# Weight conversion in one VectorE pass, wider loads, a second u buffer and later stores in a fused attention and SoLU kernel

## Chip, cores and metric

The kernel runs on one core of a Trainium2 chip. The metric is the device time of one execution in microseconds (us). All arithmetic is float32; the two weight matrices arrive as 64-bit floats and are converted on the chip.

## The reference

```python
# attention: batch 8, heads 8, seq 576, head_dim 64
scores = scale * q @ k^T                              # 576 x 576 for each head
thresh = max(scores) - tau
scores = where(scores >= thresh, scores, -1e9)
attn   = exp(scores - max) / (sum + 1e-9)
a      = attn @ v
# bridge: (B, H, S, D) -> x of 4608 tokens x 512
h   = x @ w_in                                        # 4608 x 1024
sm  = exp(h - max(h)) / (sum + 1e-9)
u   = h * sm
ln  = (u - mean(u)) / sqrt(var(u) + 1e-6) * g_ln
out = ln @ w_out                                      # 4608 x 512
```

## The kernel before

The five engines are TensorE (PE, matmuls), VectorE (DVE), ScalarE (ACT), GpSimd (POOL) and SyncE (SP, which issues most DMA transfers). Each works through its own queue in the order in which the program emits the instructions. The program is one loop over rounds `rnd`; the order inside a round is written out by hand, and lists (`begin`, `middle`, `late`, `load_at`) hold jobs for later rounds.

The first 144 rounds (`NS`) each take one attention slot: 128 query rows of two heads. PE makes the scores (L401), DVE the row maxima (L417), ACT a threshold ramp (L432) and the exponentials (L442), all on the same two PSUM tiles, so the scores of the next round wait for the ramp of this one. One round later POOL divides by the row sums (`normalise`, L449 to L452) and DVE transposes the result in blocks of 32 into T (`blocks`, L464). After every second slot SP moves T into wT with four SBUF to SBUF transfers (L475), and three or more rounds later PE multiplies with v (`attend`, L500).

When a group of tokens is complete, its feed-forward tiles (36 in all, 128 tokens each) run between the slots: h on PE in two halves (L543, L552); in `late` of that round the max hm (L565, DVE) and the exponential into u (`ff_exp`, L571, ACT); a round later the product h * u (L577, DVE); then statistics (L592, L593, DVE), small scalar work (L596 to L603, POOL), one normalised copy into V (L613, ACT) and one in u itself (L618, DVE). `ff_swap` exchanges 32-row blocks by four transfers from u into V (L629), `ff_turn` transposes V into uT (L640, DVE), and PE multiplies uT by w2 into o (L652) in two rounds. `ff_out` copies o to ob (L670, ACT) and stores it with two transfers (L676). There is one u buffer and one V buffer. After round 144 only feed-forward tiles are left; then uT alternates between two buffers.

The weights are converted in the first 16 rounds, one piece x of 128 x 512 per round: pieces 0 to 7 are w_in, 8 to 15 w_out. Three raw buffers hold pieces as they arrive. `weight_load(x + 3)` is emitted in round x: one transfer for w_in (L203), four of 32 rows for w_out (L208), each `piece(x)[0][r, g]` of the view

```python
w_rows = w_out.rearrange("(g c r x) n -> c r g x n", g=2, r=2, x=32)
```

`weight_a(x + 1)`, in round x, takes the exponent and the mantissa bits apart on DVE (L219, L225) and scales the exponent on ACT (L224). `weight_b(x)` joins low word and mantissa (L239) and sign and exponent (L242) on DVE. `weight_c(x)`, one round later, multiplies by the unit (L251) and by the power of two (L254) on POOL. `weight_d(x)`, two rounds after `weight_b`, copies a w2 piece with its halves exchanged (L261); `w2_done` after the last one allows the first o. In round 2, g_ln is turned into a column by PE (L175, L176).

`load_v` brings v for four heads: each half of the partitions gets all 512 main tokens, in two transfers of 256 tokens (L146), and the last 64 tokens (L150). Both halves hold the same data; `attend` uses the lower half for one pair of heads and the upper half for the other.

Of the kernel before, what the change touches and what calls it, by code (L numbers as in the profile page):

```python
# [8 lines left out]
F32 = mybir.dt.float32  # L9
# [4 lines left out]
ALU = mybir.AluOpType  # L14
AX = mybir.AxisListType
PSUM = bass.MemoryType.PSUM
P = 128
# [3 lines left out]
def kernel(  # L21
# [27 lines left out]
    nc = tc.nc  # L49
    B, H, S, D = q.shape  # L50
    DM, DFF = w_in.shape
    SM = 512
# [6 lines left out]
    ROWS = (slice(0, 64), slice(64, P))  # L59
# [21 lines left out]
    wide = w_in.dtype == I64  # L81
# [12 lines left out]
    ffn = {}  # L94
# [43 lines left out]
    def load_v(b, hf):  # L138
        d = halves.setdefault((b, hf), {})
        hs = slice(4 * hf, 4 * hf + 4)  # L140


        d["v"] = loads.tile([P, 4, NK, D], F32, tag="v", bufs=3, name="v")
        for rows in ROWS:
            for r in range(2):
                nc.sync.dma_start(  # L146
                    out=d["v"][rows, :, 4 * r : 4 * r + 4].rearrange("p h t d -> p h (t d)"),
                    in_=v[b, hs, 256 * r : 256 * r + 256, :].rearrange("h (p t) d -> p h (t d)", t=4),
                )
            nc.sync.dma_start(  # L150
                out=d["v"][rows, :, NK - 1], in_=v[b, hs, SM:S, :].rearrange("h p d -> p h d")
            )
# [33 lines left out]
    def piece(x):  # L186
        if x < 2 * NP:
            c, hf = divmod(x, 2)
            cols = slice(512 * hf, 512 * hf + 512)
            return w_in[P * c : P * c + P, cols], w1[:, c, cols], W_UNIT  # L190
        c = x - 2 * NP
        return w_rows[c], w2[:, 2 * c], gs[:, c : c + 1]
# [4 lines left out]
    def weight_load(x):  # L197
        raw = work.tile(
            [P, 512], I64 if wide else F32, tag=("xh2", "xh3", "uT")[x % 3], bufs=1, name="raw"
        )  # L200
        queue = nc.scalar if x < 3 else nc.sync
        if x < 2 * NP:
            queue.dma_start(out=raw, in_=piece(x)[0])  # L203
        else:
            for r in range(2):
                for g in range(2):
                    o = 64 * r + 32 * g
                    queue.dma_start(out=raw[o : o + 32], in_=piece(x)[0][r, g])  # L208
        raws[x] = dict(raw=raw)

    def weight_a(x):
# [16 lines left out]
        )  # L228

    def weight_b(x):  # L230
        d = raws[x]
        _, dst, unit = piece(x)
        if not wide:
            nc.vector.tensor_scalar(out=dst, in0=d["raw"], scalar1=unit, scalar2=None, op0=ALU.mult)
            return
        words = d["raw"].bitcast(I32).rearrange("p (n two) -> p n two", two=2)
        lo, hi = words[:, :, 0], words[:, :, 1]
        e, m = d["em"]
        nc.vector.scalar_tensor_tensor(  # L239
            out=dst, in0=lo.bitcast(U32), scalar=2.0**-32, in1=m, op0=ALU.mult, op1=ALU.add  # L240
        )
        nc.vector.scalar_tensor_tensor(  # L242
            out=e, in0=hi, scalar=-(2**31), in1=e, op0=ALU.bitwise_and, op1=ALU.bitwise_or
        )

    def weight_c(x):
        d = raws.pop(x)
        _, dst, unit = piece(x)
        if not wide:
            return  # L250
        nc.gpsimd.tensor_scalar(  # L251
            out=dst, in0=dst, scalar1=unit, scalar2=1.0, op0=ALU.mult, op1=ALU.mult
        )
        nc.gpsimd.tensor_tensor(out=dst, in0=dst, in1=d["em"][0].bitcast(F32), op=ALU.mult)  # L254


    def weight_d(x):
        c = x - 2 * NP
        if c >= 0:
            for r in range(2):  # L260
                nc.sync.dma_start(out=w2[ROWS[r], 2 * c + 1], in_=w2[ROWS[1 - r], 2 * c])  # L261
# [217 lines left out]
    def attend(key):  # L479
        b, kind, hp = key  # L480
        unit = units[key]
        wT = unit["wT"]
        unit["y"] = take("pv")
        _, y = unit["y"]
        y = y.rearrange("p (u n) -> p u n", u=2)

        for e in range(2) if kind == 2 else [None]:
            for m in range(NK):
                for u in range(2):
                    d, h0 = source(b * NP + (hp if e is None else e + 2 * u))  # L490
                    for h in range(2):
                        if e is None:
                            to = y[ROWS[h], u, 0:P].rearrange("p (r g x) -> p g r x", r=2, g=2)
                            rhs = wT[ROWS[u], :, m, :, h]
                        else:
                            to = y[ROWS[h], u, 64 * e : 64 * e + 64].rearrange(
                                "p (g x) -> p g x", g=2
                            )
                            rhs = wT[ROWS[u], :, m, e, h]
                        nc.tensor.matmul(  # L500
                            out=to, lhsT=d["v"][ROWS[u], h0 + h, m], rhs=rhs,
                            start=m == 0, stop=m == NK - 1,
                        )

# [61 lines left out]

    def ff_exp(t):
        d = ffn[t]
        d["u"] = work.tile([P, DFF], F32, tag="u", bufs=1, name="u")
        d["se"] = small.tile([P, 1], F32, tag="se", name="se")  # L570
        nc.scalar.activation(  # L571
            out=d["u"], in_=d["h"], func=AF.Exp, bias=d["nm"], scale=1.0, accum_out=d["se"]
        )
# [59 lines left out]

    def ff_turn(t, rnd):
        d = ffn[t]

        turns.append(t)
        tag = "xh0" if rnd > NS and len(turns) % 2 else "uT"
        d["uT"] = uT = work.tile([P, 2 * NC, 2, 32], F32, tag=tag, bufs=1, name="uT")
        nc.vector.transpose(  # L640
            out=uT, in_=d["V"].rearrange("p y (m x) -> p m y x", x=32)
        )
        d["turned"] = rnd + 1
# [13 lines left out]
                    )  # L657

    def ff_out(t):
        d = ffn.pop(t)  # L660
        ob = work.tile([P, DM], F32, tag="ob", name="ob")
        if len(t) == 1:
            rows = out.rearrange("(b s) m -> s b m", s=S)[SM:S, 2 * t[0] : 2 * t[0] + 2]
        else:
            b, kind, m = t
            rows = out[b * S : b * S + SM, :].rearrange("(p t) m -> t p m", t=4)
            rows = rows[2 * kind + m].rearrange("(r k) m -> k r m", r=2)


        nc.scalar.copy(  # L670
            out=ob.rearrange("p (r n) -> p r n", r=2),
            in_=d["o"].rearrange("p (r n) -> p r n", r=2)[:, :, 0:256],
        )
        pairs_free.append(d["otag"])
        for z in range(2):
            nc.sync.dma_start(  # L676
                out=rows[:, :, 256 * z : 256 * z + 256],
                in_=ob[ROWS[z]].rearrange("p (r n) -> p r n", r=2),
            )


# [34 lines left out]
    with tc.manual_schedule():  # L716
# [20 lines left out]
        rnd = 0  # L737
        prev = cur = None

        between, turns = [], []  # L740
        quarter = 0
        w2_done = False

# [1 line left out]
        while True:  # L745
# [45 lines left out]
                whole_pair(whole[rnd])  # L791
            if rnd - 1 in live:
                normalise(rnd - 1)
            if rnd - 1 in pieces:
                weight_c(pieces[rnd - 1])
            for job in middle.pop(rnd, []):
                job()
            due = bool(pv_due) and pv_due[0][0] <= rnd
# [16 lines left out]
            if step == ("h", 0):  # L815
                ff_h(cur, 0, rnd + 1 < NS)
                quarter = 1
            elif step == ("h", 1):
                ff_h(cur, 1, None)
                quarter = 2  # L820
                late.setdefault(rnd, []).append(lambda t=cur: (ff_max(t), ff_exp(t)))
                late.setdefault(rnd + 1, []).append(lambda t=cur: (ff_mul(t), ff_sum(t)))
                middle.setdefault(rnd + 2, []).append(lambda t=cur: ff_stats(t))
                late.setdefault(rnd + 2, []).append(lambda t=cur: ff_norm(t))
                middle.setdefault(rnd + 3, []).append(lambda t=cur: (ff_norm2(t), ff_swap(t)))
                late.setdefault(rnd + 4, []).append(lambda t=cur, at=rnd + 4: ff_turn(t, at))
                if not more:
                    between.append(cur)
                    cur = None
                    quarter = 0  # L830
            elif step == ("o", 0):
                if prev is not None:
                    ff_o(prev, 0)
                quarter = 3
            elif step == ("o", 1):
                if prev is not None:
                    ff_o(prev, 1)
                    begin.setdefault(rnd + 1, []).append(lambda t=prev: ff_out(t))
                prev, cur = cur, None
                quarter = 0  # L840
            if attending is not None:
# [13 lines left out]
            if rnd in pieces:  # L855
# [3 lines left out]
                    weight_load(x + 3)  # L859
                if x + 1 < len(pieces):  # L860
                    weight_a(x + 1)
            if rnd - 2 in pieces:
                weight_d(pieces[rnd - 2])
                w2_done = pieces[rnd - 2] == NW - 1
            rnd += 1


# [31 lines left out]
```

## Time and profile before

| | |
|---|---|
| median of the runs (lowest to highest) | 950.66 us (950.09 to 955.52, 3 runs) |
| the profiled execution | 941.12 us |
| its span in the profile | 939.3 us |
| PE busy | 857.3 us (91%) |
| DVE busy | 676.2 us (72%) |
| ACT busy | 667.9 us (71%) |
| POOL busy | 482.5 us (51%) |
| DMA, mean | 165 GB/s |
| mean granted PE clock | 0.964 |

The times in the profile come from one execution. A group line shows line, engine, operation, output and input with their shapes, how often, the summed busy time, the mean, and the idle time of the engine before it with what ended it. A timeline line shows start, duration, engine, line and operation, and in brackets the idle time before it. A DMA line shows how many transfers, their size, and the median time from issue to landing. "SPq" is an instruction on SP that issues a transfer; its duration includes a wait for what it needs where there is one.

### The profile page before, as it was taken

To read this page: it belongs to the slowest core of one execution; us is meant where nothing else is said; L and a number is where in the kernel's file an instruction comes from. 1 tells how busy PE (TensorE), PEld (TensorE's weight loads), DVE (VectorE), ACT (ScalarE), POOL (GpSimd) and SP (SyncE) were. 2 spreads that over 40 slices of the span, in tenths; PEclk is the share of its full clock that TensorE was granted. 3 is DMA by queue.
4 is the path that set the end of the run, shared out by engine and by line. 5 is a ranking of instruction groups with operands and counts; after the bars stand their busy time and mean duration, and the time that the engine had idled before them with its cause. 6 is when DMAs were issued, how large, how long until landed. Compare 5 with 4: busy or idle time off the path is not lost. (4 is left out here: it accounts for less than half of the span.)

```text
span 939.3 us, 39742 instructions
## 1 busy us (share of the span) xinstructions
PE 857.3 (91%) x17089; PEld 640.0 (68%) x17089; DVE 676.2 (72%) x999; ACT 667.9 (71%) x1531; POOL 482.5 (51%) x902
## 2 busy tenths in 40 slices
PE   4558689999999999999999999989999999999984
PEld 2335477868677777756587787768788777775643
DVE  4888977778677777677777777677777778876240
ACT  5868777887677778778777777768777778874111
POOL 2786864545545555545545555445545555554110
PEclk8779889999999999999999999999999999999997
DMA  9898968966889657955888657955888656855101
GB/s 241 191 243 231 225 154 204 214 149 131 189 187 203 143 142 185 229 125 126 193 184 207 141 144 170 239 129 126 188 187 207 143 126 148 183 126 124 36 24 45
DMA packets 96135, 154.62 MB, mean 165 GB/s; under 512 B 27864, under 2 KB 69848, under 8 KB 95960
## 3 DMA queue, kind: packets, MB, share of 16 engines
q1 hardware_dynamic: 94728, 150.13, 69.7%
q8 instruction: 134, 2.20, 1.0%
q10 hardware_dynamic: 1232, 1.97, 0.7%
q14 instruction: 41, 0.34, 0.1%
HBM read 46.14 MB, written 9.44 MB: 59 GB/s over the span
## 5 line engine op out<-in xcount | busy, mean ns | idle before, releaser
L417 DVE TENSOR_REDUCE nm<-s_ps 128x1 f32<-128x576 f32 x288 | 204.6, 751 | 144.9 <-PE s_ps L401 144.1
L652 PE MATMUL o_ps<-w,uT 64*64 64x256 f32 x4608 | 277.0, 384 | 17.7 <-DVE uT L640 17.3
L652 PEld LDWEIGHTS o_ps<-w,uT 64*64 64x64 f32 x4608 | 227.6, 136 | 76.3 <-issue 30.5
L432 ACT ACTIVATE w<-s_ps,nth 128x576 f32<-128x576 f32 x288 | 213.4, 741 | 19.2 <-POOL se L583 0.4
L452 POOL TENSOR_SCALAR w<-w,sm 128x576 f32<-128x576 f32 x288 | 217.4, 766 | 14.4
L552 PE MATMUL h_ps<-w,xh 64*64 64x512 f32 x1856 | 220.5, 593 | 2.1 <-issue 2.1
L442 ACT ACTIVATE w<-w,ntau 128x576 f32<-128x576 f32 x288 | 219.1, 764 | 0.0
L464 DVE STREAM_TRANSPOSE T<-w 128x576 f32<-128x576 f32 x288 | 205.7, 750 | 7.3 <-POOL w L452 7.0
L401 PE MATMUL s_ps<-kT,qT 64*64 64x64 f32 (+1 forms) x2048 | 176.1, 423 | 25.0 <-ACT w L432 22.6
L500 PEld LDWEIGHTS pv<-wT,v 64*64 64x64 f32 x5760 | 169.0, 136 | 36.3 <-issue 17.0
L449 POOL TENSOR_SCALAR sm<-sm 128x2 f32<-128x2 f32 x144 | 35.5, 247 | 284.4 <-ACT w L442 281.0
L552 PEld LDWEIGHTS h_ps<-w,xh 64*64 64x64 f32 x1856 | 115.4, 134 | 91.0 <-issue 64.6
L500 PE MATMUL pv<-wT,v 64*64 64x128 f32 (+1 forms) x5760 | 169.8, 263 | 8.2 <-DMA wT<-T 6.3
L428 ACT ACTIVATE nth<-nm,tau_t 128x1 f32<-128x1 f32 x288 | 84.5, 293 | 85.3 <-DVE nm L417 84.8
L450 POOL TENSOR_TENSOR sm<-sm,mone 128x2 f32<-128x2 f32 x144 | 102.3, 710 | 12.0
L401 PEld LDWEIGHTS s_ps<-kT,qT 64*64 64x64 f32 x2048 | 66.0, 138 | 36.0 <-ACT w L432 31.0
L640 DVE STREAM_TRANSPOSE uT<-V 128x1024 f32<-128x1024 f32 x36 | 44.6, 1239 | 49.7 <-DMA V<-u 49.6
L571 ACT ACTIVATE u<-h_ps,hm 128x1024 f32<-128x1024 f32 x36 | 40.2, 1115 | 43.3 <-DVE hm L565 37.1
L613 ACT ACTIVATE V<-u,nb,rs 128x1024 f32<-128x1024 f32 x36 | 44.6, 1240 | 35.1 <-POOL nb L603 35.1
L442 ACT ACTIVATION_READ_ACCUMULATOR w<-w,ntau 128x1 f32 x288 | 54.7, 190 | 0.0
L521 ACT COPY xh<-pv 128x256 f32<-128x256 f32 x64 | 23.5, 367 | 38.1 <-PE pv L500 37.9
L577 DVE TENSOR_TENSOR u<-h_ps,u 128x1024 f32<-128x1024 f32 x36 | 42.8, 1190 | 10.4 <-ACT u L571 10.4
(75 smaller groups left out, 671.0 us busy)
## 6 DMA issues: line engine op xcount, KB each, us to landing
wT<-T SPq DMA_DIRECT2D x288, 288.0 KB, 5.7
v<-in_v_dram SPq DMA_DIRECT2D x64, 256.0 KB, 6.8
V<-u SPq DMA_DIRECT2D x144, 64.0 KB, 2.8
out_dram<-ob SPq DMA_DIRECT2D x72, 128.0 KB, 4.6
q<-in_q_dram SPq DMA_DIRECT2D x15, 512.0 KB, 7.8
k<-in_k_dram SPq DMA_DIRECT2D x15, 512.0 KB, 7.1
raw<-in_moe_w_out_dram SPq DMA_DIRECT2D x32, 128.0 KB, 4.6
raw<-in_moe_w_in_dram SPq DMA_DIRECT2D x5, 512.0 KB, 9.5
```

Of the source, the lines that this page charges most:

```text
L401: nc.tensor.matmul(out=ps[h][ROWS[y], ks], lhsT=lhsT, rhs=d["kT"][ROWS[h], ks], start=True, stop=True,)
L417: nc.vector.tensor_reduce(out=nm, in_=ps[:, 0:S], axis=AX.X, op=ALU.max, negate=True)
L428: nc.scalar.activation(out=nth, in_=d["nth"][x], func=AF.Identity, bias=tau_t, scale=1.0)
L432: nc.scalar.activation(out=w, in_=ps[:, 0:S], func=AF.Prelu, bias=nth, scale=1.0, alpha=1.0e30,)
L442: nc.scalar.activation(out=w, in_=w, func=AF.Exp, bias=ntau, scale=1.0, accum_out=sm[:, x : x + 1])
L450: nc.gpsimd.tensor_tensor(out=sm, in0=sm, in1=mone, op=ALU.pow)
L452: nc.gpsimd.tensor_scalar(out=w, in0=w, scalar1=sm[:, x : x + 1], scalar2=1.0, op0=ALU.mult, op1=ALU.mult)
L464: nc.vector.transpose(out=T[:, :, r, h, :], in_=w)
L500: nc.tensor.matmul(out=to, lhsT=d["v"][ROWS[u], h0 + h, m], rhs=rhs, start=m == 0, stop=m == NK - 1,)
L552: mm = nc.tensor.matmul(out=h[ROWS[y], f], lhsT=x[ROWS[r], c, ROWS[y]], rhs=w1[ROWS[r], c, f], start=part == 0 and c == 0, stop=part == 1 ...
L613: nc.scalar.activation(out=V, in_=u, func=AF.Identity, bias=nb, scale=rs)
L652: nc.tensor.matmul(out=d["o"][ROWS[z], 512 * r : 512 * r + 256], lhsT=d["uT"][ROWS[r], m].rearrange("p y x -> p (y x)"), rhs=w2[ROWS[r], m ...
```

## The change

A w_out piece is loaded by two transfers of 64 rows in place of four of 32. v is loaded by one transfer over all 128 partitions and two over 64, in place of four over 64; the upper half then holds the two groups of 256 tokens in exchanged order, and `attend` picks them with `m ^ 4 * u`. The last step of the conversion is one DVE instruction in `weight_b`; `weight_c` is gone, and `weight_d` runs one round sooner. In rounds after 144, u alternates between its buffer and that of `xh1`. There, while more tiles are ready to start, `ff_turn` is emitted two rounds later. The store is split from `ff_out` and emitted in `late` of the same round, behind the block transfers.

```diff
--- before.py
+++ after.py
@@ -141,12 +141,14 @@
 
 
         d["v"] = loads.tile([P, 4, NK, D], F32, tag="v", bufs=3, name="v")
+        rest = v[b, hs, 0:SM, :].rearrange("h (p t) d -> p h (t d)", t=4)
+        for to, rows, of in (
+            (0, slice(0, P), slice(0, P)), (4, ROWS[0], ROWS[1]), (4, ROWS[1], ROWS[0])
+        ):
+            nc.sync.dma_start(
+                out=d["v"][rows, :, to : to + 4].rearrange("p h t d -> p h (t d)"), in_=rest[of]
+            )
         for rows in ROWS:
-            for r in range(2):
-                nc.sync.dma_start(
-                    out=d["v"][rows, :, 4 * r : 4 * r + 4].rearrange("p h t d -> p h (t d)"),
-                    in_=v[b, hs, 256 * r : 256 * r + 256, :].rearrange("h (p t) d -> p h (t d)", t=4),
-                )
             nc.sync.dma_start(
                 out=d["v"][rows, :, NK - 1], in_=v[b, hs, SM:S, :].rearrange("h p d -> p h d")
             )
@@ -203,9 +205,7 @@
             queue.dma_start(out=raw, in_=piece(x)[0])
         else:
             for r in range(2):
-                for g in range(2):
-                    o = 64 * r + 32 * g
-                    queue.dma_start(out=raw[o : o + 32], in_=piece(x)[0][r, g])
+                queue.dma_start(out=raw[ROWS[r]], in_=piece(x)[0][r])
         raws[x] = dict(raw=raw)
 
     def weight_a(x):
@@ -228,7 +228,7 @@
         )
 
     def weight_b(x):
-        d = raws[x]
+        d = raws.pop(x)
         _, dst, unit = piece(x)
         if not wide:
             nc.vector.tensor_scalar(out=dst, in0=d["raw"], scalar1=unit, scalar2=None, op0=ALU.mult)
@@ -242,16 +242,9 @@
         nc.vector.scalar_tensor_tensor(
             out=e, in0=hi, scalar=-(2**31), in1=e, op0=ALU.bitwise_and, op1=ALU.bitwise_or
         )
-
-    def weight_c(x):
-        d = raws.pop(x)
-        _, dst, unit = piece(x)
-        if not wide:
-            return
-        nc.gpsimd.tensor_scalar(
-            out=dst, in0=dst, scalar1=unit, scalar2=1.0, op0=ALU.mult, op1=ALU.mult
-        )
-        nc.gpsimd.tensor_tensor(out=dst, in0=dst, in1=d["em"][0].bitcast(F32), op=ALU.mult)
+        nc.vector.scalar_tensor_tensor(
+            out=dst, in0=dst, scalar=unit, in1=e.bitcast(F32), op0=ALU.mult, op1=ALU.mult
+        )
 
 
     def weight_d(x):
@@ -498,7 +491,8 @@
                             )
                             rhs = wT[ROWS[u], :, m, e, h]
                         nc.tensor.matmul(
-                            out=to, lhsT=d["v"][ROWS[u], h0 + h, m], rhs=rhs,
+                            out=to, lhsT=d["v"][ROWS[u], h0 + h, m ^ 4 * u if m < 8 else m],
+                            rhs=rhs,
                             start=m == 0, stop=m == NK - 1,
                         )
 
@@ -566,7 +560,10 @@
 
     def ff_exp(t):
         d = ffn[t]
-        d["u"] = work.tile([P, DFF], F32, tag="u", bufs=1, name="u")
+
+        starts.append(t)
+        tag = "xh1" if rnd > NS and len(starts) % 2 else "u"
+        d["u"] = work.tile([P, DFF], F32, tag=tag, bufs=1, name="u")
         d["se"] = small.tile([P, 1], F32, tag="se", name="se")
         nc.scalar.activation(
             out=d["u"], in_=d["h"], func=AF.Exp, bias=d["nm"], scale=1.0, accum_out=d["se"]
@@ -633,7 +630,6 @@
 
     def ff_turn(t, rnd):
         d = ffn[t]
-
         turns.append(t)
         tag = "xh0" if rnd > NS and len(turns) % 2 else "uT"
         d["uT"] = uT = work.tile([P, 2 * NC, 2, 32], F32, tag=tag, bufs=1, name="uT")
@@ -657,25 +653,28 @@
                     )
 
     def ff_out(t):
+        d = ffn[t]
+        d["ob"] = ob = work.tile([P, DM], F32, tag="ob", name="ob")
+
+
+        nc.scalar.copy(
+            out=ob.rearrange("p (r n) -> p r n", r=2),
+            in_=d["o"].rearrange("p (r n) -> p r n", r=2)[:, :, 0:256],
+        )
+        pairs_free.append(d["otag"])
+
+    def ff_store(t):
         d = ffn.pop(t)
-        ob = work.tile([P, DM], F32, tag="ob", name="ob")
         if len(t) == 1:
             rows = out.rearrange("(b s) m -> s b m", s=S)[SM:S, 2 * t[0] : 2 * t[0] + 2]
         else:
             b, kind, m = t
             rows = out[b * S : b * S + SM, :].rearrange("(p t) m -> t p m", t=4)
             rows = rows[2 * kind + m].rearrange("(r k) m -> k r m", r=2)
-
-
-        nc.scalar.copy(
-            out=ob.rearrange("p (r n) -> p r n", r=2),
-            in_=d["o"].rearrange("p (r n) -> p r n", r=2)[:, :, 0:256],
-        )
-        pairs_free.append(d["otag"])
         for z in range(2):
             nc.sync.dma_start(
                 out=rows[:, :, 256 * z : 256 * z + 256],
-                in_=ob[ROWS[z]].rearrange("p (r n) -> p r n", r=2),
+                in_=d["ob"][ROWS[z]].rearrange("p (r n) -> p r n", r=2),
             )
 
 
@@ -737,7 +736,7 @@
         rnd = 0
         prev = cur = None
 
-        between, turns = [], []
+        between, starts, turns = [], [], []
         quarter = 0
         w2_done = False
 
@@ -791,8 +790,6 @@
                 whole_pair(whole[rnd])
             if rnd - 1 in live:
                 normalise(rnd - 1)
-            if rnd - 1 in pieces:
-                weight_c(pieces[rnd - 1])
             for job in middle.pop(rnd, []):
                 job()
             due = bool(pv_due) and pv_due[0][0] <= rnd
@@ -823,7 +820,9 @@
                 middle.setdefault(rnd + 2, []).append(lambda t=cur: ff_stats(t))
                 late.setdefault(rnd + 2, []).append(lambda t=cur: ff_norm(t))
                 middle.setdefault(rnd + 3, []).append(lambda t=cur: (ff_norm2(t), ff_swap(t)))
-                late.setdefault(rnd + 4, []).append(lambda t=cur, at=rnd + 4: ff_turn(t, at))
+
+                at = rnd + 4 if more or not ready else rnd + 6
+                late.setdefault(at, []).append(lambda t=cur, at=at: ff_turn(t, at))
                 if not more:
                     between.append(cur)
                     cur = None
@@ -836,6 +835,7 @@
                 if prev is not None:
                     ff_o(prev, 1)
                     begin.setdefault(rnd + 1, []).append(lambda t=prev: ff_out(t))
+                    late.setdefault(rnd + 1, []).append(lambda t=prev: ff_store(t))
                 prev, cur = cur, None
                 quarter = 0
             if attending is not None:
@@ -859,9 +859,9 @@
                     weight_load(x + 3)
                 if x + 1 < len(pieces):
                     weight_a(x + 1)
-            if rnd - 2 in pieces:
-                weight_d(pieces[rnd - 2])
-                w2_done = pieces[rnd - 2] == NW - 1
+            if rnd - 1 in pieces:
+                weight_d(pieces[rnd - 1])
+                w2_done = pieces[rnd - 1] == NW - 1
             rnd += 1
```

## The prediction

> **What bounds the kernel now.** I read the page first, then busy time by stretch, the waits, the timelines of the stretches where TensorE (PE) idles, and the DMA view of the stage that the loads touch.
>
> ```profile
> span 939.3 us, 39742 instructions
> PE 857.3 (91%) x17089; PEld 640.0 (68%) x17089; DVE 676.2 (72%) x999; ACT 667.9 (71%) x1531; POOL 482.5 (51%) x902
> PE   4558689999999999999999999989999999999984
> POOL 2786864545545555545545555445545555554110
> ```
>
> Three stages. From 140 to 838 us PE is full (682 of 698 us). In the head (0 to 140 us) it idles 50 us; there GpSimd (POOL) is busiest. In the tail it idles 17 us. So work moved between other engines counts only in head and tail, and in the middle only where it makes PE wait.
>
> ```profile
> 20.00:48.00 28.00, 16.02 (x297) 9.96 (x297) 24.43 (x37) 22.89 (x56) 22.53 (x27) 0.72 0.89 193
> 48.00:60.00 12.00, 7.02 (x104) 4.74 (x104) 11.48 (x18) 8.80 (x20) 10.19 (x14) 0.72 1.09 247
> 60.00:80.00 20.00, 10.79 (x230) 8.78 (x234) 14.13 (x23) 11.90 (x31) 12.81 (x17) 0.74 0.89 219
> 80.00:110.00 30.00, 21.91 (x382) 13.47 (x378) 28.63 (x44) 23.12 (x56) 25.91 (x36) 0.89 0.95 237
> ```
>
> Columns: PE, PEld, DVE, ACT, POOL busy, PE clock, DMA share, GB/s. Where the sixteen weight pieces are converted, one per round, VectorE (DVE) and the DMA engines are both nearly full; each round's first pass on DVE (L219) needs the next piece landed, and DVE works in order, so a late piece stops scores, transposes and PE behind it. The w_out pieces are x = 8 to 15, loaded from 48.6 us (L208); L219 for the last runs at 107.1 us.
>
> ```profile
> GB/s 255 245 242 242 251 246 246 233 242 259 244 257 264 256 274 226 228 158 238 229 265 215 195 68 170 269 389 263 251 242 250 249 274 212 164 154 184 191 237 283
> DMA packets 6748, 13.57 MB, mean 234 GB/s; under 512 B 2018, under 2 KB 4067, under 8 KB 6738
> raw<-in_moe_w_out_dram SPq DMA_DIRECT2D x32, 128.0 KB, 4.6
> ```
>
> These are for 44 to 102 us: 13.57 MB, of which w_out is 32 x 128 KB = 4.19 MB. The best slice moved 389 GB/s, 24.3 GB/s for each of 16 engines.
>
> Tail, DVE and PE:
>
> ```profile
> 885.09 0.81 DVE L618 TENSOR_SCALAR u<-u,rs,nb 128x1024 f32<-128x1024 f32 x1 [2.30 <-ACT V L613]
> 891.90 1.25 DVE L640 STREAM_TRANSPOSE uT<-V 128x1024 f32<-128x1024 f32 x1 [5.99 <-DMA V<-u]
> 893.07 1.18 DVE L565 TENSOR_REDUCE hm<-h_ps 128x1 f32<-128x1024 f32 x1
> ...
> 909.18 8.82 PE L652 MATMUL o_ps<-w,uT 64*64 64x256 f32 x128 [4.06 <-DVE uT L640]
> 925.14 9.37 PE L652 MATMUL o_ps<-w,uT 64*64 64x256 f32 x128 [7.13 <-DVE uT L640]
> ```
>
> The h of the fourth tail tile is complete at 883.9 us (PE), yet its max (hm) starts at 893.07, because uT of the tile before stands ahead of it on DVE and waits 6 us for the block swap V<-u. The same repeats one tile on. PE then waits 4.06 and 7.13 us and runs slowly after each pause.
>
> **What the Trainium skill says.** "DMA: Bandwidth & Descriptors", section "Why a DMA increments its semaphore by 16 and not by 1": a transfer issued from SP or ACT runs on k engines, the largest k up to 16 that divides the slowest dimension (other than 1) of both sides; the lowest-numbered k. This trace agrees where it can: the g_ln load, 8 partitions from a source with outer size 16, left 9 completion records (8 engines, and one jump for the rest), every other transfer a multiple of 16. "SBUF — State Buffer", section "Who interferes with whom": a DVE instruction with two SBUF inputs and a GpSimd one reading SBUF exclude each other. The trace agrees: L242 takes 0.68 us alone and 1.76 beside POOL's L254.
>
> **The change, part by part.**
>
> (1) w_out loads. Each piece becomes 2 transfers of 256 KB in place of 4 of 128 KB. In the built program the old source is 32 rows by 512, its target 32 partitions: k = 16. The new source is 2 x 32 x 512 (g stays its own dimension, since its rows lie far apart), the target 64 partitions: the largest k dividing 2 and 64 is 2. All sixteen transfers then go through the same two engines, 4.19/2 = 2.1 MB each. At 24.3 GB/s that is 86 us; at the stage's mean, 234/16 = 14.6 GB/s, 143 us. The same two engines carry 1/16 of everything else: 13.57 - 4.19, less some 1.5 MB before 48.6 us and w_in's rest, is 7.9 MB, 0.49 MB each, 20 to 34 us. I take the fast end, as the other fourteen engines will be half empty: 106 us. Three raw buffers and eight completion counters on SP let two or three pieces stand in the queue, so these engines don't run dry. Start 48.6, landing lag 2 (half of the 4.6 us above): the last piece lands at 157 us, where L219 wants it at 107.1. Cost: +50 us (upper end, 177 us: +121). No other work hides it: DVE needs every piece in order, and scores, wT and pv of each round follow DVE. If the rule did not hold, this part costs nothing and saves SP 16 issues of 0.4 us.
>
> (2) Conversion. POOL loses L251 (0.67 us mean) and L254 (1.52) per piece, 35 us in all. DVE gains a third two-input pass; L239 and L242 alone take 0.65 and 0.68, so 16 x 0.65 = +10.4. It loses the exclusion: L242 averages 1.223, so 16 x (1.223 - 0.68) = -8.7, and L239 16 x (0.755 - 0.65) = -1.7, L219 and L225 -1.3 by their means over 0.42. Sum: -1.3. From both sides: if POOL's remaining L452 held the pass up as L254 held L242, 1.76 each, +17.8 more; if pieces are late anyway, 0. I take -1. The e buffer, which POOL's L254 released, is now released by DVE: no wait there before or after. SP's w2 half-swap (L261) goes out one round sooner, so w2 is ready one round sooner: by the order of instructions one attention round now comes after the first o-matmuls instead of before. PE idles 1.96 + 0.55 us there (122 to 125 us): -2.5.
>
> (3) Middle. SP held V<-u back behind v loads and a store:
>
> ```profile
> 603.18 1.28 SPq L146 DMA_DIRECT2D v<-in_v_dram  x2
> 604.51 1.16 SPq L150 DMA_DIRECT2D v<-in_v_dram  x1
> 605.77 1.32 SPq L676 DMA_DIRECT2D out_dram<-ob  x2
> 607.19 3.57 SPq L629 DMA_DIRECT2D V<-u  x4
> ...
> 613.65 3.68 PE L652 MATMUL o_ps<-w,uT 64*64 64x256 f32 x64 [3.10 <-DVE uT L640]
> ```
>
> The store moves behind V<-u and the wT transfers (1.3 us earlier for V<-u), and v needs 5 issues in place of 6 (0.65 us earlier; the 128-partition load has k = 16). So V<-u starts 2 us sooner. PE waited 2.87, 0.17 and 3.10 us for uT in the middle, with slow matmuls after the first (5.01 us for 64 in place of 3.7); 2 + 0.2 + 2 + 1 = -5.2. Behind the store stand only later loads, whose buffers are wanted rounds later: nothing.
>
> (4) Tail. DVE runs max, product and statistics of a tile before uT of the tile before it, and the exponential writes the other u. Replayed with measured steps: norm2 of tile 3 ends at 885.9; hm of tile 4 follows at once (h since 883.9), 7.2 us sooner. From hm: exp +1.26, product +2.50, statistics end +5.30, nb +7.38, V ends +8.66, norm2 ends +9.50, swap landed +3.9 (four issues of 0.57 and landing; the store is behind it), uT 1.25. Tile 4: statistics end 891.2; uT of tile 3 till 892.5, in time for PE at 898.0; V, norm2 till 895.4, swap 899.3. Tile 5: its h ends at 898.0; statistics end 903.35, uT of tile 4 till 904.65 (PE wants it at 905.05), norm2 ends 907.55, swap 911.5, uT 912.8. PE: o of tile 4 ends 912.1, o of tile 5 912.85 + 7.3 = 920.2 in place of 934.5. With copy and store: -14.4. Late next is the chain of the last tile from its h on, so no more is to be had here.
>
> **Sum.** +50 - 1 - 2.5 - 5.2 - 14.4 = +27. The profiled execution took 941.12 us (span 939.3 and 1.8 around it): 968. The median of the runs is 950.66, 9.5 us above it; I add the 27 to the median: 978.
>
> **Rivals.** (a) The loads use all engines, or four. For it: nothing in the trace shows a two-engine transfer, and the rule was seen at work once. The part decides the sign from a last landing of 130 us (a delay of 23); with k = 4 it is 1.05 MB or 43 us + 20, landing at 114, so any k of 4 or more ends faster. With 16: 950.66 - 23 = 927.6, say 928. (b) As (a), but DVE's new pass is held up by POOL: +17.8, 945. Against: L452 falls beside the max, which took 0.75 us with it. (c) Two engines at the crowded rate: +121 - 23, 1048. Against: that mean had all sixteen engines pulling at once.
>
> **Numbers.** The measurement tells about 1% from no change. Forecast 0.72; (a) 0.13, (b) 0.03, (c) 0.12, spread from 1000 up. Forecast's own range 955 to 1015 (last landing at 134 to 194 us); with most of (c) 955 to 1035, which leaves out (a), (b) and the end of (c). Faster 0.13, same 0.05, slower 0.82.
>
> **What would show it.** Right: 256 KB w_out loads that take 15 us or more to land instead of 4.6; DVE waiting for raw 40 us or more; the last L219 pass near 157 us; DMA GB/s under 150 in 50 to 150 us; the o-waits of 4.06 and 7.13 us gone, and PE's last matmul some 14 us nearer to the last scores. Wrong: landings of 5 us, and a head as long as before or shorter.

## The result, and the profile after

The changed kernel takes 984.03 us (median of 4 runs, 980.61 to 988.47); the kernel before took 952.85 us beside it (4 runs). The ratio is 1.033, with an interval of 1.0273 to 1.0388. The forecast was 978, in a range of 955 to 1035. The profiled execution took 980.61 us, with a span of 978.8.

The page of the changed kernel, busy tenths in 40 slices of 24.5 us:

```profile
span 978.8 us, 39719 instructions
PE 865.4 (88%) x17089; PEld 654.3 (67%) x17089; DVE 677.0 (69%) x1015; ACT 669.0 (68%) x1531; POOL 447.8 (46%) x870
PE   4634734999998999998999999999999999999997
POOL 1440222455455545554555545554554555566210
DMA  8863444789758785788578956796588866666511
GB/s 245 194 151 91 129 113 111 158 205 227 153 126 201 195 199 124 175 199 182 122 171 175 211 125 140 188 238 153 129 186 180 208 143 138 153 140 126 123 47 45
```

PE's row reads 3 4 7 3 4 in slices 3 to 7 (49 to 171 us), where it used to climb, and is full only from slice 8 on. In slices 4 to 7 the DMA share is down to 3 and 4 tenths, at 91 to 129 GB/s; before had 0.78 to 0.95 and 177 to 237 GB/s from 80 to 140 us. So the head became longer while everything in it became emptier, the sign of a narrow supply. At the right end PE's row ends in 997 where before it ended in 984: the tail became denser. By stretch (columns PE, PEld, DVE, ACT, POOL busy, PE clock, DMA share, GB/s):

```profile
48.00:120.00 72.00, 35.14 (x534) 24.52 (x530) 32.95 (x56) 29.61 (x74) 18.38 (x29) 0.67 0.47 122
120.00:180.00 60.00, 27.91 (x362) 17.25 (x358) 28.96 (x47) 24.82 (x58) 14.47 (x24) 0.66 0.50 130
```

DVE, which was nearly full in 80 to 110 us before, is half idle. What it waits for in the first 180 us, from the waits (us in total, times, longest), and the last of these passes in the timeline:

```profile
DVE em L219 <- DMA raw<-in_moe_w_out_dram: 67.0, 8, 13.8
168.27 0.43 DVE L219 TENSOR_SCALAR em<-raw 128x512 int32<-128x512 int32 x1 [9.40 <-DMA raw<-in_moe_w_out_dram]
```

The same of the kernel before:

```profile
DVE em L219 <- DMA raw<-in_moe_w_out_dram: 2.4, 1, 2.4
107.14 0.41 DVE L219 TENSOR_SCALAR em<-raw 128x512 int32<-128x512 int32 x1
```

And the DMA view of 44 to 165 us, share in tenths and GB/s in 40 slices of 3 us:

```profile
DMA  9993165891118921111165466934114792116824
GB/s 203 235 286 92 50 173 98 166 226 60 58 51 186 201 74 58 53 51 53 60 130 194 80 169 143 232 86 125 53 53 124 146 235 73 53 51 157 212 69 131
```

DVE waited once for each of the eight w_out pieces, 67.0 us in all, and the last L219 pass runs at 168.27 us where it ran at 107.14. In the DMA rows the reader should look for the floor: whenever nothing but w_out is in flight, the share is 1 tenth and the rate 50 to 53 GB/s. Two engines of sixteen are an eighth, and 51/2 is 25.5 GB/s each, about the 24.3 that the best slice of before gave an engine. This is the k = 2 that the Trainium skill's rule gave ("DMA: Bandwidth & Descriptors", "Why a DMA increments its semaphore by 16 and not by 1"). The profile gives no landing time for these loads, so the landings of 15 us or more, one of the signs that the prediction named, can't be read.

The tail in the timeline of the changed kernel, PE and then DVE:

```profile
902.85 3.70 PE L537 MATMUL h_ps<-w,xh 128*128 128x512 f32 x8
...
937.66 7.14 PE L648 MATMUL o_ps<-w,uT 64*64 64x256 f32 x128
944.73 7.13 PE L537 MATMUL h_ps<-w,xe 128*128 128x512 f32 x16
951.79 14.04 PE L648 MATMUL o_ps<-w,uT 64*64 64x256 f32 x256
966.87 7.14 PE L648 MATMUL o_ps<-w,uT 64*64 64x256 f32 x128 [1.03 <-DVE uT L636]
...
938.40 0.81 DVE L615 TENSOR_SCALAR u<-u,rs,nb 128x1024 f32<-128x1024 f32 x1 [2.31 <-ACT V L610]
939.13 1.22 DVE L559 TENSOR_REDUCE hm<-h_ps 128x1 f32<-128x1024 f32 x1
944.38 1.25 DVE L636 STREAM_TRANSPOSE uT<-V 128x1024 f32<-128x1024 f32 x1
```

The fourth tile's h ends at 937.7 and its hm starts at 939.13, straight behind norm2 (L615) and ahead of uT (L636) of the tile before. The waits of 4.06 and 7.13 us for uT have become none and 1.03, and the matmuls behind them run at full rate: from the first matmul of the tail's last four tiles (the first L537, at 902.85) to the end of the span it is 75.95 us. In the kernel before, from the same matmul, it was 90.25:

```profile
849.05 3.70 PE L543 MATMUL h_ps<-w,xh 128*128 128x512 f32 x8
```

So the difference of the two spans, 39.5 us, splits in three: +61.1 up to the last L219 pass, -14.3 in the tail from that first matmul on, and -7.3 between.

### The profile page after: what moved, and what is told of

Read it like the earlier page. It is cut to its first block, busy times and chain, and to the rows that moved or that the text cites. A ratio compares the mean times of both kernels' runs of the same rounds, so it can differ in the third digit from the quotient of the medians.

```text
span 978.8 us, 39719 instructions
## 1 busy us (share of the span) xinstructions
PE 865.4 (88%) x17089; PEld 654.3 (67%) x17089; DVE 677.0 (69%) x1015; ACT 669.0 (68%) x1531; POOL 447.8 (46%) x870
## 5 line engine op out<-in xcount | busy, mean ns | idle before, releaser
L648 PE MATMUL o_ps<-w,uT 64*64 64x256 f32 x4608 | 270.4, 378 | 5.1 <-DVE uT L636 5.1
L648 PEld LDWEIGHTS o_ps<-w,uT 64*64 64x64 f32 x4608 | 230.5, 134 | 53.0 <-issue 16.0
L546 PE MATMUL h_ps<-w,xh 64*64 64x512 f32 x1856 | 223.0, 598 | 2.7 <-issue 2.7
L445 POOL TENSOR_SCALAR w<-w,sm 128x576 f32<-128x576 f32 x288 | 217.3, 767 | 14.3
L493 PEld LDWEIGHTS pv<-wT,v 64*64 64x64 f32 x5760 | 174.3, 139 | 59.5 <-issue 39.8
L493 PE MATMUL pv<-wT,v 64*64 64x128 f32 (+1 forms) x5760 | 177.0, 268 | 27.5 <-DMA wT<-T 26.6
L394 PE MATMUL s_ps<-kT,qT 64*64 64x512 f32 (+1 forms) x2048 | 178.7, 431 | 23.8 <-ACT w L425 21.2
L546 PEld LDWEIGHTS h_ps<-w,xh 64*64 64x64 f32 x1856 | 117.6, 136 | 92.8 <-issue 65.2
L394 PEld LDWEIGHTS s_ps<-kT,qT 64*64 64x64 f32 x2048 | 68.2, 142 | 32.2 <-ACT w L425 27.9
L636 DVE STREAM_TRANSPOSE uT<-V 128x1024 f32<-128x1024 f32 x36 | 44.1, 1225 | 19.7 <-DMA V<-u 19.7
L515 ACT COPY xh<-pv 128x256 f32<-128x256 f32 x64 | 23.4, 366 | 48.7 <-PE pv L493 48.6
L219 DVE TENSOR_SCALAR em<-raw 128x512 int32<-128x512 int32 x16 | 6.8, 423 | 67.0 <-DMA raw<-in_moe_w_out_dram 67.0
```

Source lines behind the costliest of these rows:

```text
L394: nc.tensor.matmul(out=ps[h][ROWS[y], ks], lhsT=lhsT, rhs=d["kT"][ROWS[h], ks], start=True, stop=True,)
L445: nc.gpsimd.tensor_scalar(out=w, in0=w, scalar1=sm[:, x : x + 1], scalar2=1.0, op0=ALU.mult, op1=ALU.mult)
L493: nc.tensor.matmul(out=to, lhsT=d["v"][ROWS[u], h0 + h, m ^ 4 * u if m < 8 else m], rhs=rhs, start=m == 0, stop=m == NK - 1,)
L546: mm = nc.tensor.matmul(out=h[ROWS[y], f], lhsT=x[ROWS[r], c, ROWS[y]], rhs=w1[ROWS[r], c, f], start=part == 0 and c == 0, stop=part == 1 ...
L648: nc.tensor.matmul(out=d["o"][ROWS[z], 512 * r : 512 * r + 256], lhsT=d["uT"][ROWS[r], m].rearrange("p y x -> p (y x)"), rhs=w2[ROWS[r], m ...
```

## The experiments

The kernels ran in three groups, each with runs of the kernel before on the same chip, whose medians were 952.41, 952.37 and 950.54 us.

**The loads.** First the changed kernel without its w_out part, and the kernel before with that part alone.

```diff
 # e1_narrow: changed kernel
-                queue.dma_start(out=raw[ROWS[r]], in_=piece(x)[0][r])
+                for g in range(2):
+                    o = 64 * r + 32 * g
+                    queue.dma_start(out=raw[o : o + 32], in_=piece(x)[0][r, g])
 # e2_wide_only: kernel before
-                for g in range(2):
-                    o = 64 * r + 32 * g
-                    queue.dma_start(out=raw[o : o + 32], in_=piece(x)[0][r, g])
+                queue.dma_start(out=raw[ROWS[r]], in_=piece(x)[0][r])
```

> The changed kernel with the old w_out loads: four transfers of 32 rows for each piece. Two-engine theory: the whole loss is in these loads. DVE waits for w_out pieces under 8 us in place of 67; the last L219 pass comes near 105 us in place of 168.3; the time is 984 - 61 = 923 us (918 to 930), so 25 to 30 us under the kernel before. Rival (the loss comes from the third DVE pass, from the second u buffer or from the later stores): still 975 us or more.

> The kernel before with only the w_out loads of the change: two transfers of 64 rows for each piece. Two-engine theory: the last L219 pass moves from 107 to 165 us or later, and the time is 952 + 60 = 1012 us (1003 to 1022). Rival (the loads cost only together with the DVE pass or the store order): under 985 us. Rival (the loss comes from the other parts): 952 us.

e1_narrow: 929.0 us (0.9783, 0.9723 to 0.9842). e2_wide_only: 1008.77 us (1.0607, 1.0552 to 1.0662). DVE's wait in e2_wide_only, from the waits:

```profile
DVE em L217 <- DMA raw<-in_moe_w_out_dram: 72.9, 8, 15.4
```

Its last pass in the timeline:

```profile
169.51 0.43 DVE L217 TENSOR_SCALAR em<-raw 128x512 int32<-128x512 int32 x1 [9.51 <-DMA raw<-in_moe_w_out_dram]
```

And its rates from 44 to 165 us in the DMA view:

```profile
GB/s 213 245 242 174 66 54 199 111 214 150 56 54 77 222 160 57 54 46 47 51 60 170 78 193 76 202 188 93 82 51 53 133 172 231 49 51 60 206 171 47
```

Nearly the same floor (about 50 GB/s) and the same last pass, with nothing else changed: the two wide loads per piece cost 56.4 us alone and 55.0 (984.03 less 929.0) in company. The rest of the change gains some 23 us. The sign of the whole is the sign of this one part.

Then the number of engines itself. A piece comes as one transfer over 128 partitions, and only the shape of the source differs. The rows of w2 then stand in another order, which the rest of these three kernels doesn't follow: they time the load and are no versions to use.

```diff
 # e3_k4, e9_k8, e4_k16: changed kernel; (a, x) = (4, 32), (8, 16), (16, 8)
-    w_rows = w_out.rearrange("(g c r x) n -> c r g x n", g=2, r=2, x=32)
+    w_rows = w_out.rearrange("(a c x) n -> c a x n", a=4, x=32)
...
-            for r in range(2):
-                queue.dma_start(out=raw[ROWS[r]], in_=piece(x)[0][r])
+            queue.dma_start(out=raw, in_=piece(x)[0])
```

> The changed kernel with one transfer of 128 rows for each w_out piece, whose source is 4 groups of 32 neighbouring rows; so the rows of w2 stand in another order than the reference's, with the same work. Two-engine theory, by the rule for the number of engines: slowest dimensions 4 and 128, so four engines with 1.05 MB each, 40 us at 26 GB/s and some 20 us for the rest: the last piece lands near 110 us; 930 us (922 to 940). Rival (wide transfers are slow by their size, 512 KB in one here): 984 us or more.

> As the one with 4 groups, but the source is 16 groups of 8 neighbouring rows (w2's rows again in another order). Two-engine theory: sixteen engines, nothing left of the loss, 923 us (917 to 929), no slower than with four loads of 32 rows. Rival (wide transfers are slow by their size): 984 us or more. Rival (the number of groups in the source makes it slower, not the engines): slower than with 4 groups.

> The changed kernel with a w_out piece as one transfer over 128 partitions from a source of 8 groups of 16 rows (the rows of w2 then stand in another order). Theory, now fitted to k = 2 and 4: each of the k engines has 1024/k rows of 4096 bytes at 0.159 us, and its sixteenth of all other transfers of that stage, 39 us; at k = 2 that is 81 + 39 = 120 us (measured from the first w_out load to the last L219 pass 119.7), at k = 4 41 + 39 = 80 (83.0). At k = 8 it is 20 + 39 = 59, the 58.5 us that before has there: last L219 pass at 107 to 110 us, 930 (925 to 936). Rival (the loss grows with every step below 16 engines, as 26 us at k = 4 would suggest): last pass at 115 us or later, 937 or more.

| source | us | ratio (interval) | last pass em<-raw (L219, in the others L218) | DVE's waits for w_out |
|---|---|---|---|---|
| 2 groups (changed kernel) | 984.03 | 1.033 (1.0273 to 1.0388) | 168.3 | 67.0, 8 times |
| 4 groups (e3_k4) | 957.15 | 1.0041 (1.0014 to 1.0068) | 131.6 | 26.9, 6 times |
| 8 groups (e9_k8) | 936.06 | 0.9875 (0.9829 to 0.9921) | 119.4 | 13.7, 3 times |
| 16 groups (e4_k16) | 931.4 | 0.9803 (0.9747 to 0.9859) | 109.2 | 2.1, once |

The ladder is in order, and with four groups the floor doubles. The DMA rows of e3_k4 for 44 to 135 us:

```profile
DMA  9999695998995222358694795837943952889727
GB/s 244 242 254 231 166 233 116 202 194 216 222 202 113 103 106 105 131 163 238 144 272 101 130 199 119 220 114 184 206 79 114 211 107 97 233 246 220 127 94 161
```

Between the other transfers the share is now 2 and 3 tenths and the rate 103 to 106 GB/s, four times 26.

The packets tell the number of engines without the rates. Each row of w_out is one packet of 4096 bytes, and the traces show how many of these are under way at the same moment. In the changed kernel it is two for 80 of the 96 us in which there is any, and more than two for 3.8 us. In e3_k4 it is four for 41 of 63 us, in e9_k8 it is most often eight, and in the kernel before and in e4_k16 it reaches sixteen and more. The completion records, one for each engine that has done its part, agree: e1_narrow left 11064 of them and the changed kernel 10601, 463 fewer. Thirty-two transfers of sixteen records against sixteen of three (two engines and one jump, counted as for g_ln in the prediction) make 464 fewer.

The time of e3_k4, though, was expected at 930 and came out at 957, and e4_k16 at 931.4 lies above its expected 917 to 929. So the working of the load time, in the prediction and here, had an error that the next runs had to find.

**Why the loads were slower than worked out.** The last pass came 11 us later than the 157 of the prediction. One suspect was SP: in the changed kernel it waits up to 5.6 us at L208 for an earlier w_out load, with wT and the half exchange queued behind it, and there are four pauses, 20.1 us in all, in which no w_out packet is in flight (the expectation below puts them at 24). e8_act_queue takes the w_out loads off SP.

```diff
 # e8_act_queue: changed kernel
-        queue = nc.scalar if x < 3 else nc.sync
+        queue = nc.sync if 3 <= x < 2 * NP else nc.scalar
```

> The changed kernel with the w_out loads issued from ACT in place of SP, the transfers themselves as they are (64 partitions, two engines each). Theory (the load term came out at 61 and not 50 us because SP, which waits up to 5.9 us to issue such a load and has wT, the half exchange and more behind it, lets the two engines run dry for about 24 us in all): the pauses shrink, the last L219 pass moves from 168 to about 157 us, and the run takes about 973. Rival (the pauses are the other traffic of those two engines, or the three raw buffers): last pass at 166 to 170 us, 984.

It took 988.33 us (1.0408, 1.0343 to 1.0474), with the last pass at 170.25. The pauses did go: no gap between w_out packets is longer than 0.41 us. The waits of SP (44 to 170 us) and of DVE (0 to 180 us) in e8_act_queue:

```profile
SPq L254 <- DMA raw<-in_moe_w_out_dram: 34.5, 6, 8.1
SPq L468 <- DMA raw<-in_moe_w_out_dram: 32.9, 5, 8.2
...
DVE em L219 <- DMA raw<-in_moe_w_out_dram: 46.4, 8, 9.3
DVE em L242 <- ACT em L224: 18.6, 4, 6.7
```

SP's other transfers now stand in front of or behind w_out, and part of DVE's wait has gone over to the exponent pass (L242 for L224) that stands behind the loads on ACT. But with a w_out packet in flight nearly all the time, the last one ends at 169.7 us, where in the changed kernel it ended at 167.7. So the pauses in SP's queue don't explain the late landing. They were not empty time either: at no moment of them was no packet under way, and in the two long ones, of 8.0 and 7.4 us, the sixteen engines were on average 76% and 68% busy.

What fills the engines is seen in the packets of the changed kernel that start between the first w_out load (48.1 us) and the last L219 pass (168.3), by size:

```
bytes   packets    MB   median ns   packets x median / 16 engines
 4608      1085   5.00     281      19.1 us
 4096      1152   4.72     159      (1024 of them w_out)
 1024      2951   3.02      46       8.5 us
 2048       632   1.29     148       5.8 us
  256      1024   0.26      18       1.2 us
all but the 4096                    35.4 us (with 0.8 of other sizes)
```

Each of the two engines carries half of the 1024 w_out rows, 512 x 0.159 = 81.4 us, and, taken as an even share, a sixteenth of the rest, 35.4 us: together 116.8, against 120.2 us measured between the two points. The same with each run's own packets and its own two points:

| run | w_out rows of one engine | the rest | sum | measured |
|---|---|---|---|---|
| 2 groups (changed kernel) | 512 x 0.159 = 81.4 | 35.4 | 116.8 | 120.2 |
| 4 groups (e3_k4) | 256 x 0.161 = 41.2 | 36.9 | 78.1 | 83.2 |
| 8 groups (e9_k8) | 128 x 0.2545 = 32.6 | 41.5 | 74.1 | 71.4 |
| 16 groups (e4_k16) | 64 x 0.274 = 17.5 | 39.7 | 57.2 | 60.7 |

e9_k8 was run as the test of this sum, and its expectation missed: it took the 0.159 us of two engines for eight (and 39 us for the rest) and gave 59 us, where 71.4 was measured and the last pass came 10 us later than expected. The rival's numbers for that run (115 us or later) hold for the pass; 936.06 lies at the border of the two. With the run's own packets the sum comes to 74.1, so most of the miss is the packet time: in e9_k8 a w_out row took 0.159 us when no other data packet was under way during it, and 0.294 with fourteen or more (medians). Why rows get slower side by side is open. The sum stays an estimate, from medians and even shares, good to some 5 us here.

**The other parts, each alone on the kernel before.**

```diff
 # e5_tail
-        d["u"] = work.tile([P, DFF], F32, tag="u", bufs=1, name="u")
+        starts.append(t)
+        tag = "xh1" if rnd > NS and len(starts) % 2 else "u"
+        d["u"] = work.tile([P, DFF], F32, tag=tag, bufs=1, name="u")
...
+                at = rnd + 4 if more or not ready else rnd + 6
 # e6_conv: weight_c and its call are gone, weight_d at rnd - 1; in weight_b
+        nc.vector.scalar_tensor_tensor(
+            out=dst, in0=dst, scalar=unit, in1=e.bitcast(F32), op0=ALU.mult, op1=ALU.mult
+        )
 # e7_store_v: ff_store split off and put in late, v in five transfers
 # e11_store: the same without the v loads
```

> Before plus the tail's part alone: two u buffers after the last scores and uT two rounds later there. Theory (step 4 of the prediction): 14.4 us less than before, from the waits of 4.06 and 7.13 us for uT, which go, and the slow matmuls behind them; from the start of the fourth tail tile's h to the end about 76 us in place of 90.25; 938 where before runs 952.4. Rival (the chain of the last tile from its h on sets the end in any case): 952 with the two waits moved elsewhere in the tail.

> Before plus the conversion's part alone: the last multiplication as one DVE pass, none on POOL, w2's half exchange one round sooner. Theory (step 2): DVE's L242 falls from 1.223 to about 0.68 us and the new pass of about 0.7 us takes back what that saves (-1), and the first o comes a round sooner (-2.5): 949 where before runs 952.4. Rival (b): the new pass is held up by POOL as L242 was, about 1.76 us each, +17.8: 970.

> Before plus the store behind the block transfers and the v loads in five issues, nothing else. Theory (step 3): the block swap V<-u starts about 2 us sooner where v loads and a store stood before it, and PE's waits for uT between the slots (2.87, 0.17, 3.10 us and slow matmuls) go: 5.2 us less, 947 where before runs 952.4. Rival: SP's queue has slack elsewhere and the wait only moves: 952.

> Before plus the store behind the block transfers, the v loads as they were. Theory: of the 10.8 us of both, some 3.5 are in the tail, where the store stood before V<-u, and two thirds of the 5.2 in the middle (1.3 us of the 2 by which V<-u comes sooner): 945.5. Rival (the v loads carry the gain, since they fill SP in front of wT too): 950 or more.

| part alone | us | ratio (interval) | against before |
|---|---|---|---|
| e5_tail | 939.31 | 0.9873 (0.9837 to 0.991) | -13.1 |
| e6_conv | 953.84 | 1.0022 (1.0001 to 1.0043) | +1.5 |
| e7_store_v | 941.53 | 0.9899 (0.9852 to 0.9945) | -10.8 |
| e11_store | 940.69 | 0.99 (0.9872 to 0.9928) | -9.9 |

e7_store_v gained twice what was expected of it: some 3.5 us of the 10.8 are in the tail, which its expectation left out. e11_store gained 9.9 us where some 7 were expected. e5_tail and e7_store_v shorten the tail, counted from the first L543 (L546) as above, from 90.25 us to 77.1 and 86.8. The end of e5_tail on PE, in the timeline:

```profile
913.96 14.04 PE L654 MATMUL o_ps<-w,uT 64*64 64x256 f32 x256
930.17 7.14 PE L654 MATMUL o_ps<-w,uT 64*64 64x256 f32 x128 [2.16 <-DVE uT L642]
```

The same of e7_store_v:

```profile
914.14 7.14 PE L657 MATMUL o_ps<-w,uT 64*64 64x256 f32 x128 [0.95 <-DVE uT L645]
929.23 9.80 PE L657 MATMUL o_ps<-w,uT 64*64 64x256 f32 x128 [7.95 <-DVE uT L645]
```

With the tail's part alone (second u buffer and later uT, which were not taken apart) only 2.16 us of waiting are left. With the store behind V<-u alone the first wait falls from 4.06 to 0.95 and the second stays. Both together give 75.95, so some 2.3 us of the two gains are the same pause. The v loads add nothing that can be told from noise (-10.8 against -9.9).

In e6_conv the passes on DVE are those of the prediction. The group of L242 in the kernel before (busy, mean ns | idle before it):

```profile
L242 DVE SCALAR_TENSOR_TENSOR em<-raw,em 128x512 int32<-128x512 int32 x16 | 19.6, 1223 | 0.0
```

In e6_conv:

```profile
L242 DVE SCALAR_TENSOR_TENSOR em<-raw,em 128x512 int32<-128x512 int32 x16 | 11.4, 712 | 0.0
L245 DVE SCALAR_TENSOR_TENSOR w<-w,gs,em 128x512 f32<-128x512 f32 x8 | 6.0, 752 | 0.3
L245 DVE SCALAR_TENSOR_TENSOR w<-w,em 128x512 f32<-128x512 f32 x8 | 5.5, 693 | 0.3
```

L242 without POOL's two-input pass beside it takes 0.712 us, and L245 takes that saving back. The five passes of one piece add up to 47.4 us over 16 pieces, where the four of before took 46.5. Rival (b), DVE held up by POOL's L452, did not come; what POOL had done was free there, and taking it off gained nothing.

**Best version.** The last pair asked whether the conversion is worth anything in company. e10_tail_store_v is e7_store_v and e5_tail in one; e12_narrow_again is e1_narrow.

> Before plus tail, store and v loads; the conversion stays as it was, on DVE and POOL, and the w_out loads stay narrow. Theory (the parts add: 13.1 of the tail alone, 10.8 of store and v, of which some 3 are the same pause of the tail): 931. If the conversion part is worth the 3.5 us that the prediction gave it, 932.5 against 929.0 of the kernel that has it too; if it is worth nothing or costs 1.5, as measured alone, 927 to 929.

> The changed kernel with the four narrow w_out loads once more, beside the one without the conversion part: 929 (0.978 of before). Its distance to that one is the worth of the conversion part in company: -3.5 by the prediction, 0 to +1.5 by its measurement alone.

e10_tail_store_v: 929.61 us (0.9802, 0.9762 to 0.9841). e12_narrow_again: 929.4 us (0.9798, 0.9755 to 0.9842). They can't be told apart: the conversion is worth nothing that these runs can show. Either is 2.0% faster than the kernel before and 5 to 6% faster than the changed one. The changed kernel with the old four loads, or the same without the conversion, is the version to keep.

## Why the prediction was right, and which terms were off

**(1) The loads, +50: right in sign and mechanism, a tenth short.** By the medians the loads cost 55 to 56 us, and in the one profile the last L219 pass comes 61.1 us later. Of the two terms, w_out on its two engines was put at 86 us and came to 81.4 (4 KB at 0.159 us is 25.8 GB/s). The mis-sized one is the other traffic of the same engines, "7.9 MB, 0.49 MB each, 20 to 34 us", where I took the fast end: it came to 35.4. Both factors failed. The bytes are 9.7 MB without the 4096-byte packets, in a head that became longer; and they move at 17.2 GB/s per engine (0.608 MB in 35.4 us), not at 24.3. wT's packets of 4608 bytes, half of these bytes, take 281 ns, which is 16.4 GB/s. The reason for the fast end (empty neighbours) held for w_out's own rows; it said nothing about the size and kind of the other packets. That the loads "don't run dry" was not so, since w_out paused for 20.1 us, but e8_act_queue shows that the pauses didn't set the time.

**Rival (a), and with it the k of 4.** "Any k of 4 or more ends faster" was wrong: four engines took 957.15, no faster than before. The same mis-sized term did it: 43 + 20 should have landed at 114, and 41 + 37, and some 5 us that the sum doesn't hold, brought the last pass to 131.6. With sixteen, 928 was forecast and 929.0 (narrow loads) and 931.4 (one wide load) measured.

**(2) The conversion, -1 and -2.5: nothing.** The exclusion that the skill names ("SBUF — State Buffer", "Who interferes with whom") went as priced, 1.223 to 0.71 us; the passes sum to +0.9 in e6_conv in place of -1.3. The first o a round sooner brought no gain: e6_conv is 1.5 us slower than before, with an interval of 0 to 4. One reading was wrong here too: the prediction calls POOL the busiest engine of the head, but in all four lines that it shows DVE is busier than POOL (28.63 against 25.91 of 30 us in the last). So the part moved work off an engine that had room and onto the fuller one.

**(3) The middle, -5.2.** Here the profiles mislead. The middle of the changed kernel is 7.3 us shorter than that of before, as (2) and (3) summed up to, but e5_tail, whose middle is the same as before's, has it 14 us longer in its profile (755.9 against 741.9 us, from the last L219 pass to the tail's first matmul): one execution's middle can't carry a few us. The medians can: e11_store gains 9.9 (7 to 12 by its interval), of which 3.4 are in the tail by its own profile (86.9 in place of 90.25), which leaves some 6 for the middle. The forecast's 5.2 was about right; its split, with a third for the v loads, was not shown.

**(4) The tail, -14.4: right.** Measured -14.3 in the profile of the changed kernel, and by the steps of the replay: hm straight behind norm2, uT of tile 3 in time, the last wait 1.03 us where 0.75 was forecast (912.85 less 912.1). e5_tail alone gains 13.1.

**The sum.** +61.1 - 7.3 - 14.3 = +39.5 between the two profiled executions, where +27 was forecast; between the medians it is 31.2, because the profiled execution of before lay well below its median and that of the changed kernel only 3.4 us below. So the 12.5 us by which the terms of the profiles miss are in good part the difference of two single executions. By the medians the loads are +55 to +56 where +50 was forecast, and all the rest is -23.4 (e1_narrow) or -21.1 (e12_narrow_again) where -23.1 was forecast. That the rest came out so near is in part luck: the 3.5 us of the conversion were not there, and the middle gave somewhat more than forecast.

## What to carry to other kernels

Before making transfers fewer and wider, look at the outermost dimension of both sides in the built program: here a source cut in two groups put the whole load on two engines, though its target had 64 partitions. Price such a load as its rows on those engines plus their share of everything else in that stage, with packet times taken where as many packets are under way. In a tail with one tile after another, let the first steps of a tile stand ahead of the last step of the tile before, and stores behind the transfers that the next matmul waits for.

## What the runs showed of the hardware that was not expected

- One engine moved 4 KB rows at 25 to 26.5 GB/s, alone or beside three others of its kind: the floors were 50 to 53 GB/s with two groups and 103 to 106 with four.
- The same row took 0.159 us on two engines and 0.161 on four, but 0.2545 on eight and 0.274 on sixteen (medians of the changed kernel, e3_k4, e9_k8 and e4_k16).
- A queue of its own (ACT in place of SP) did not help a load whose engines were full: 988.33 against 984.03 us, though the pauses between the loads, 20.1 us, were gone.
